# Raw weight pieces in four places instead of three, with every engine's instructions laid in a new order

## The chip, the cores and the metric

The kernel runs on one core of a Trainium2 chip. The metric is the device time of one execution in microseconds (us), the lower the better. A core has five engines that run side by side and wait for each other through semaphores: TensorE (PE; PEld is its weight load), VectorE (DVE), ScalarE (ACT), GpSimd (POOL) and SyncE (SP, which only issues the transfers here). SBUF is the on-chip memory and PSUM the memory that PE writes.

## The reference

Attention over 768 positions (4 batches, 8 heads, head size 64) with a band of 96 positions and 8 global ones, and behind it a feed-forward layer of 512 to 2048 to 512 with a piecewise quadratic in place of a GELU:

```python
scores = 0.125 * q @ k.T - slope * dist          # kept where global or local, else -1e9
a = softmax(scores)                              # by row
x = (a @ v) laid out as (4 * 768, 512)
h = x @ w_in                                     # 3072 x 2048
g = where(h >= 1, h, where(h <= -1, 0, (h + 1) ** 2 / 4))
out = g @ w_out                                  # 3072 x 512
```

w_in and w_out come as 64-bit floats, everything else as 32-bit floats.

## The kernel before

**Work.** The rows are cut into 24 units of 128 (one block of one batch) and 12 chunks of two units. A unit's attention is `scores` (PE), `masked` (DVE), `expo` and `split_p` (ACT, DVE), a transposing transfer `turn_p`, `attend` (PE), `scale_x`, `split_x` and `turn_x`. The first four units take another path (`first_...`) in which everything is in 32 bits. For a chunk c and a group g of 256 of the 2048 inner columns come `ffn1` (PE, 24 matmuls into a PSUM tile h), `gelu` (ACT step 0, DVE steps 1 and 2, then ACT and POOL), and `ffn2` (chunks 0 to 2) or `first_products` and `last_products` (later chunks, which use sums and differences of w_out that `diff` makes). Each 32-bit factor is split into a high and a low 16-bit part, so a product takes three matmuls.

**The weights.** w_in and w_out come in 32 pieces of 512 KB, 16 each. Piece n is loaded by `w_load` (an SP transfer) as raw 64-bit words into one of three places of the tile `wd`, `n % 3`. Then `w_bits` makes 32-bit floats of it: on DVE a first step (L532), a second one (L536, or for the pieces marked "s" in `WS`, which are 2, 5, 8, 11 and 14, an ACT step, L534) and a third one (L540). The first two write a PSUM tile (`w_bits`, or `spare` for the odd pieces of w_in), the third writes the result into another part of `wd`. The "s" pieces have a POOL step more, `w_sign` (L547), which still reads the raw place. `w_hi` and `w_scale` (ACT, L553, L560) and `w_lo` (POOL, L567) then give the two 16-bit parts that PE uses. A raw place can take its next piece once the last reader of the piece in it is done: the third DVE step, or `w_sign`.

**Order.** Nothing is left to a scheduler. Every step has a number, by its time in a plan, and `PLACE` is the list of these numbers in the order in which the program is written. An engine runs its own instructions of that list in that order; SP too, so a transfer that waits for its place holds up those behind it. `SLOTS` says, for each kind of tile, which buffer each tile takes. `filler` steps are PE matmuls without use that stand where PE has nothing else to do.

`wd` has eight parts: 0 to 2 are the raw places, 3 to 6 hold the 32-bit pieces, and 7 holds `own_bias`, which the `masked` steps of the first four units read. Later `diff` writes all eight.

Of the kernel before, what the change touches and what calls it, by code (L numbers as in the profile page):

```python
# [11 lines left out]
I32 = mybir.dt.int32  # L12
# [329 lines left out]
def fast_path(ctx, tc, q, k, v, nraw, nval, w_in, w_out, out, half, one, stat, marks, badi):  # L342
# [221 lines left out]
    def w_lo(n):  # L564
        num, src, hi, lo = piece(n)
        after(("hi", n), ("scale", n))
        nc.gpsimd.tensor_sub(lo, wf[n], hi)  # L567
        did.add(("w", n))

    def put_weight(n, t, tl):  # L570
        at(tl, w_load, n)
        at(t, w_bits, n, 0)
# [910 lines left out]
```

## Time and profile before

| | |
|---|---|
| runs | 593.86 us median of 3 (592.65 to 594.44) |
| the profiled execution | 592.99 us, span of its instructions 591.1 us |
| TensorE clock granted | 1.00 up to 575 us |
| busy share of the span | PE 97%, POOL 85%, DVE 80%, ACT 74% |

Times within the profile are counted from the start of the span. PE is counted busy from the start of a matmul to a modelled end; fillers count as busy.

### The profile page before, as it was taken

What the parts mean: (1) busy time and instruction counts of PE and PEld (TensorE: products, weight loads), DVE (VectorE), ACT (ScalarE), POOL (GpSimd) and SP (SyncE); (2) the same over time, 40 slices, a digit from 0 to 9 for tenths busy, and PEclk for the clock granted to TensorE, in tenths of its full rate; (3) what the DMA queues carried; (4) which work ended last, traced back from release to release, by engine and by line L of the source; (5) the groups of instructions that cost most, each with busy time, mean ns of one, the idle gap of its engine ahead of it and who ended that gap; (6) DMA issues with size and microseconds to landing.
All of it is one profiled execution on the core that took longest, in us unless ns stands there. A gap on an engine that the chain in (4) does not pass through costs nothing.

```text
span 591.1 us, 16452 instructions
## 1 busy us (share of the span) xinstructions
PE 571.7 (97%) x6243; PEld 475.7 (80%) x6243; DVE 473.5 (80%) x1175; ACT 440.2 (74%) x1146; POOL 502.2 (85%) x570
## 2 busy tenths in 40 slices
PE   7998999899999999999999999999999999999995
PEld 5876764457768688988888889888889889898884
DVE  8998999999884788787987987888979877874321
ACT  5998898998866798776976877868868768635340
POOL 0888999879999999899899998799899799579780
PEclk9999999999999999999999999999999999999999
DMA  7875675694840557848865777767667677250001
GB/s 248 279 247 189 203 238 185 144 173 88 191 105 2 114 129 153 179 127 197 196 160 129 171 176 155 179 172 188 169 150 170 158 172 171 56 123 1 2 37 42
DMA packets 144235, 88.19 MB, mean 149 GB/s; under 512 B 108180, under 2 KB 124820, under 8 KB 144148
## 3 DMA queue, kind: packets, MB, share of 16 engines
q1 hardware_dynamic: 144144, 87.05, 59.1%
q8 instruction: 51, 0.84, 0.6%
q14 instruction: 36, 0.29, 0.2%
q10 hardware_dynamic: 4, 0.00, 0.0%
HBM read 54.53 MB, written 6.29 MB: 103 GB/s over the span
## 4 chain that ended last, share of the span: by engine, by line
PE 66%; DVE 11%; ACT 10%; DMA 5%; POOL 4%; issue 3%; ACTq 0%; SPq 0%; DVEq 0%; POOLq 0%
PE h L939 30%; PE o L1042 26%; ACT z L644 5%; PE s L813 4%; PE av L854 4%; PE o L998 3%; DMA wd<-in_moe_w_out_dram 2%; DMA wd<-in_moe_w_in_dram 2%; DVE wd L540 2%; DVE u L964 1%; DVE h L962 1%; ACT ph L827 1%; POOL ga L972 1%; DVE w_bits L536 1%; DVE ph L829 1%
## 5 line engine op out<-in xcount | busy, mean ns | idle before, releaser
L939 PE MATMUL h<-xt,wih 128*128 128x256 f16 x1536 | 256.0, 273 | 5.0 <-DVE u L964 4.9
L939 PE MATMUL h<-xt,wil 128*128 128x256 f16 x768 | 209.3, 273 | 0.0
L939 PEld LDWEIGHTS <-wih 128*128 128x128 f16 x1536 | 148.4, 98 | 29.2 <-DVE u L964 9.9
L962 DVE SCALAR_TENSOR_TENSOR h<-h,u 128x512 f32<-128x512 f32 x96 | 66.4, 692 | 42.1 <-ACT u L958 41.6
L644 ACT ACTIVATE z<-z,stat 128x256 f32<-128x256 f32 (+1 forms) x192 | 91.5, 479 | 9.2 <-DVE stat L632 9.1
L983 POOL TENSOR_TENSOR ga<-u,ga 128x512 f16<-128x512 f32 x72 | 88.3, 1227 | 10.1 <-ACT ga L981 9.8
L1042 PEld LDWEIGHTS <-ga 128*128 128x128 f16 x864 | 83.2, 98 | 10.0
L958 ACT ACTIVATE u<-h,half 128x512 f32<-128x512 f32 x96 | 65.1, 678 | 33.0 <-PE h L939 22.6
L939 PEld LDWEIGHTS <-wil 128*128 128x128 f16 x768 | 75.2, 98 | 8.7
L974 POOL TENSOR_TENSOR u<-u 128x256 f32<-128x256 f32 x72 | 60.2, 838 | 20.0 <-DVE u L964 18.9
L988 POOL TENSOR_TENSOR gb<-u,gb 128x384 f16<-128x384 f32 x72 | 72.0, 1002 | 3.7 <-ACT gb L986 3.7
L1042 PE MATMUL o<-wd,ga 128*128 128x256 f16 x432 | 70.7, 273 | 0.0
L1042 PE MATMUL o<-woh,ga 128*128 128x256 f16 x288 | 70.7, 273 | 0.0
L1042 PEld LDWEIGHTS <-gb 128*128 128x128 f16 x648 | 62.3, 98 | 8.4 <-issue 1.0
L981 ACT ACTIVATE ga<-u 128x512 f16<-128x512 f32 x72 | 44.4, 621 | 33.2 <-POOL u L976 26.6
L964 DVE SCALAR_TENSOR_TENSOR u<-u,h 128x512 f32<-128x512 f32 x96 | 65.2, 680 | 3.6
L829 DVE SCALAR_TENSOR_TENSOR ph<-z,ph 128x1024 f16<-128x1024 f32 x40 | 57.0, 1428 | 9.4 <-ACT ph L827 9.0
L632 DVE CUSTOM_DVE_ANT_0 z<-s,bias 128x256 f32<-128x256 f32 x160 | 59.1, 414 | 5.1 <-PE s L813 4.7
L998 PE MATMUL o<-woh,ga 128*128 128x512 f16 x192 | 61.4, 379 | 0.6 <-ACT ob L1115 0.6
L1042 PE MATMUL o<-wd,gb 128*128 128x256 f16 x432 | 60.6, 273 | 0.8 <-DVE ob L1093 0.8
L998 PEld LDWEIGHTS <-ga 128*128 128x128 f16 x288 | 27.3, 98 | 30.6 <-issue 2.2
L599 DVE TENSOR_REDUCE stat<-c_raw 128x1 f32<-128x256 f32 x128 | 48.5, 406 | 4.3 <-DMA c_raw<-in_moe_w_in_dram 4.3
(132 smaller groups left out, 1172.2 us busy)
## 6 DMA issues: line engine op xcount, KB each, us to landing
wd<-in_moe_w_in_dram SPq DMA_DIRECT2D x16, 512.0 KB, 4.5
wd<-in_moe_w_out_dram SPq DMA_DIRECT2D x16, 512.0 KB, 4.2
c_raw<-in_moe_w_in_dram SPq DMA_DIRECT2D x32, 256.0 KB, 3.0
c_raw<-in_moe_w_out_dram SPq DMA_DIRECT2D x32, 256.0 KB, 3.4
kr<-in_k_dram SPq DMA_DIRECT2D x28, 256.0 KB, 3.6
vr<-in_v_dram SPq DMA_DIRECT2D x28, 256.0 KB, 3.6
qr<-in_q_dram SPq DMA_DIRECT2D x24, 256.0 KB, 3.9
out_dram<-ob SPq DMA_DIRECT2D x23, 256.0 KB, 3.1
```

The source lines that it names most:

```text
L632: nc.vector.tensor_tensor_reduce(out=p32[u, hf][:, hh, :], in0=pts[u, hf][hh // 2][:, hh % 2, 0:n], in1=(own_bias if n == P else bias)[:, ...
L644: nc.scalar.activation(z, z, AF.Exp, bias=nm[:, c : c + 1], scale=-1.0, accum_out=sums[:, c : c + 1])
L829: nc.vector.scalar_tensor_tensor(phs[u, hf][:, 1, :], zf, SP_, phs[u, hf][:, 0, :], op0=ALU.mult, op1=ALU.subtract)
L939: nc.tensor.matmul(hp[:, :, e, :], w[:, dc, f], xt[:, hf, 2 * a + j, :], start=(n == 0), stop=(n == 3 * NDC - 1),)
L958: nc.scalar.activation(u, h, AF.Relu, bias=half, scale=2.0 / (SV * SW), accum_out=su[:, col : col + 1])
L962: nc.vector.scalar_tensor_tensor(h, h, 4.0 / (SV * SW), u, op0=ALU.mult, op1=ALU.max)
L964: nc.vector.scalar_tensor_tensor(u, u, 4.0, h, op0=ALU.min, op1=ALU.mult)
L974: nc.gpsimd.tensor_sub(f[:, 3:7:3], f[:, 0:6:5], f[:, 4:5].to_broadcast([P, 2, P]))
L983: nc.gpsimd.tensor_sub(gas[c, g][:, 1], f[:, 0:4], gas[c, g][:, 0])
L988: nc.gpsimd.tensor_sub(gbs[c, g][:, 1, 0:3], f[:, 4:7], gbs[c, g][:, 0, 0:3])
L998: nc.tensor.matmul(po, a, w[:, f, :], start=(f == 0 and n == 0), stop=(f == NFC - 1 and n == 2))
L1042: nc.tensor.matmul(acc[:, e], x, w, start=first and n == 0, stop=last and n == 2)
```

## The change

Pieces 0 to 8 keep the three places. From the tenth piece (n = 9) on, raw pieces take four places in turn: 7, 0, 1, 2. Place 7 is the one that `own_bias` holds for the first four units. `PLACE` and `SLOTS` are new lists: all engines' instructions stand in a new order, and tiles take other buffers. The list names 36 fillers where it named 37. The other new code (`WL`, `GM`, `square`) chooses variants that the values given (`"p"` and `"d"`) never take, so that apart from the filler the instructions are the same ones.

```diff
 PLACE = [
...
-    0, 2, 1, 10, 13, 8, 20, 11, 4, 29, 3, 5, 6, 7, 89, 90, 91, 31, 15, 21, 16, 19, 18, 14, 38, 30, 39, 43, 34, 41, 26,
...
+    0, 2, 1, 10, 13, 8, 20, 11, 4, 3, 5, 6, 7, 89, 90, 91, 21, 12, 31, 9, 14, 15, 23, 22, 29, 27, 26, 25, 30, 24, 18,
...
 SLOTS = {
...
-    "raw": [int(n, 16) for n in "1001100110100110101011000110100011010010101100011010010011010100"],
+    "raw": [int(n, 16) for n in "0101010101101001010110010101100100101101000101101010001010100100"],
...
+R4 = 9
+GM = "d"
+WL = "pppppppppppppppppppppppppppppppp"
...
     def w_load(n):
         num, src, hi, lo = piece(n)
-        r = wd[:, n % 3].bitcast(I32).rearrange("p t a b -> p (t a b)")
+        r = wd[:, n % 3 if n < R4 else (7, 0, 1, 2)[(n - R4) % 4]].bitcast(I32).rearrange("p t a b -> p (t a b)")
...
     def w_lo(n):
         num, src, hi, lo = piece(n)
-        after(("hi", n), ("scale", n))
-        nc.gpsimd.tensor_sub(lo, wf[n], hi)
         did.add(("w", n))
+        if WL[n] == "v":
+            after(("hi", n))
+            nc.vector.scalar_tensor_tensor(lo, wf[n], SW, hi, op0=ALU.mult, op1=ALU.subtract)
+        else:
+            after(("hi", n), ("scale", n))
+            nc.gpsimd.tensor_sub(lo, wf[n], hi)
...
+    def square(c, g):
+        return GM[min(c * (NFC // 2) + g, len(GM) - 1)] == "s"
```

On DVE, around piece 16 (first piece of w_out), the order before has the third step of piece 13, whose place piece 16 takes, seven rows ahead of the first step of piece 16. A tile `w16_bits` belongs to piece 16; the four rows with `spare1` are the third step of piece 13 and the steps of piece 15; h and u are gelu steps.

```order
L540 SCALAR_TENSOR_TENSOR wd_117<-wd_117,spare1_172 128x512
L964 SCALAR_TENSOR_TENSOR u1_1_810<-u1_1_810,h1_1_746 128x2x256
L532 TENSOR_SCALAR w14_bits_826<-wd_117 128x512
L962 SCALAR_TENSOR_TENSOR h0_3_783<-h0_3_783,u0_3_823 128x512
L540 SCALAR_TENSOR_TENSOR wd_117<-wd_117,w14_bits_826 128x512
L532 TENSOR_SCALAR spare1_172<-wd_117 128x512
L964 SCALAR_TENSOR_TENSOR u0_3_823<-u0_3_823,h0_3_783 128x2x256
L536 SCALAR_TENSOR_TENSOR spare1_172<-wd_117,spare1_172 128x512
L532 TENSOR_SCALAR w16_bits_903<-wd_117 128x512
```

With the change piece 16 takes the place of piece 12, and on DVE the third step of piece 12 stands nine rows ahead of the first step of piece 16 (`spare1` is piece 13 here).

```order
L543 SCALAR_TENSOR_TENSOR wd_117<-wd_117,w12_bits_736 128x512
L982 SCALAR_TENSOR_TENSOR u0_2_768<-u0_2_768,h0_2_691 128x2x256
L535 TENSOR_SCALAR w14_bits_784<-wd_117 128x512
L535 TENSOR_SCALAR spare1_170<-wd_117 128x512
L980 SCALAR_TENSOR_TENSOR h1_1_740<-h1_1_740,u1_1_777 128x512
L539 SCALAR_TENSOR_TENSOR spare1_170<-wd_117,spare1_170 128x512
L982 SCALAR_TENSOR_TENSOR u1_1_777<-u1_1_777,h1_1_740 128x2x256
L543 SCALAR_TENSOR_TENSOR wd_117<-wd_117,spare1_170 128x512
L543 SCALAR_TENSOR_TENSOR wd_117<-wd_117,w14_bits_784 128x512
L980 SCALAR_TENSOR_TENSOR h0_3_790<-h0_3_790,u0_3_828 128x512
L535 TENSOR_SCALAR w16_bits_865<-wd_117 128x512
```

The first steps of pieces 16 and 15 have changed places, and the place is freed two DVE steps earlier.

On SP, from the load of piece 7 on, the order before is this; the rows named wd are the loads of the pieces, one after the other, the others are 256 KB of k, q or v of a unit.

```order
L518 DMA wd_117<-in_moe_w_in_dram 128x4x256
L746 DMA kr4_1_483<-in_k_dram 128x512
L746 DMA kr4_0_512<-in_k_dram 128x512
L518 DMA wd_117<-in_moe_w_in_dram 128x4x256 x2
L746 DMA qr4_1_599<-in_q_dram 128x512
L746 DMA vr4_0_603<-in_v_dram 128x512
L518 DMA wd_117<-in_moe_w_in_dram 128x4x256 x3
```

With the change, the same loads from piece 7 on (the first row is pieces 7 to 10, the fourth pieces 11 to 14):

```order
L521 DMA wd_117<-in_moe_w_in_dram 128x4x256 x4
L754 DMA kr5_2_552<-in_k_dram 128x512
L754 DMA qr4_1_560<-in_q_dram 128x512
L521 DMA wd_117<-in_moe_w_in_dram 128x4x256 x4
L754 DMA vr5_2_726<-in_v_dram 128x512
L754 DMA kr4_0_731<-in_k_dram 128x512
```

Four loads of pieces stand in a row, with two transfers of 256 KB right behind them, where there were one to three with two transfers between.

## Rows read from the trace of the kernel before

**Rows 1.** The head of the page, and busy time by engine.
```profile
span 591.1 us, 16452 instructions
PE   571.7 (97%) x6243; PEld 475.7 (80%) x6243; DVE 473.5 (80%) x1175; ACT 440.2 (74%) x1146; POOL 502.2 (85%) x570
```

**Rows 2.** Busy time in three stretches: length, busy us by engine, clock, DMA share, GB/s.
```profile
20.00:110.00 90.00, 82.78 (x681) 59.25 (x682) 85.06 (x184) 82.86 (x203) 81.17 (x78) 1.00 0.67 208
110.00:575.00 465.00, 463.35 (x5364) 396.50 (x5362) 367.95 (x891) 343.40 (x893) 415.83 (x483) 1.00 0.59 137
575.00:591.10 16.10, 9.70 (x89) 8.28 (x86) 2.86 (x8) 0.38 (x1) 1.36 (x2) 0.91 0.12 39
```

**Rows 3.** PE's fillers from 20 to 110 us: group of instructions, busy us, mean ns.
```profile
L494 PE MATMUL spare<-zeros 128*128 128x512 f16 x25 | 6.9, 379 | 0.0
```

**Rows 4.** PE's waits from 20 to 110 us: total us, times, longest.
```profile
PE h L939 <- DVE u L964: 3.5, 5, 1.1
PE s L813 <- DVE wd L540: 1.3, 1, 1.3
PE o L998 <- POOL wol L567: 0.6, 1, 0.6
```

**Rows 5.** PE in time, 42 to 62 us: start, length, instruction, idle before.
```profile
49.90 0.81 PE L494 MATMUL spare<-zeros 128*128 128x512 f16 x3
51.78 0.39 PE L939 MATMUL h<-xt,wih 128*128 128x256 f16 x2 [1.07 <-DVE u L964]
...
57.39 1.03 PE L494 MATMUL spare<-zeros 128*128 128x512 f16 x4
59.41 0.39 PE L939 MATMUL h<-xt,wih 128*128 128x256 f16 x2 [1.00 <-DVE u L964]
```

**Rows 6.** DVE's waits for transfers of weights, over the whole span.
```profile
DVE w_bits L532 <- DMA wd<-in_moe_w_out_dram: 2.0, 3, 1.0
DVE w_bits L532 <- DMA wd<-in_moe_w_in_dram: 1.1, 2, 0.6
DVE spare L532 <- DMA wd<-in_moe_w_in_dram: 0.8, 1, 0.8
```

**Rows 7.** DVE in time around the first step of piece 16 (56.28 us).
```profile
50.45 0.67 DVE L540 SCALAR_TENSOR_TENSOR wd<-wd,spare 128x512 int32<-128x512 int32 x1
51.05 0.67 DVE L964 SCALAR_TENSOR_TENSOR u<-u,h 128x512 f32<-128x512 f32 x1
...
54.62 0.68 DVE L536 SCALAR_TENSOR_TENSOR spare<-wd,spare 128x512 int32<-128x512 int32 x1
56.28 0.69 DVE L532 TENSOR_SCALAR w_bits<-wd 128x512 int32<-128x512 int32 x1 [0.98 <-DMA wd<-in_moe_w_out_dram]
```

**Rows 8.** The line that issues the loads of pieces: time to landing.
```profile
DMA to landing us min/median/max: 3.4/4.3/5.5
```

**Rows 9.** SP's longest wait by line: us in total, times, longest.
```profile
SPq L518 <- DVE wd L540: 42.9, 20, 3.8
```

**Rows 10.** Busy time from 20 to 40 us, columns as in rows 2.
```profile
20.00:40.00 20.00, 19.39 (x161) 15.86 (x162) 19.41 (x61) 20.00 (x60) 17.75 (x20) 1.00 0.84 270
```

**Rows 11.** POOL's `w_sign` steps from 20 to 105 us.
```profile
L547 POOL TENSOR_TENSOR wd<-wd 128x512 f32<-128x512 f32 x5 | 6.5, 1295 | 3.4 <-DVE r L656 1.4 <-ACT wd L534 1.4 <-ACT wih L553 0.6
```

**Rows 12.** All engines in time, 103 to 108 us: the steps of piece 31.
```profile
103.39 0.68 DVE L540 SCALAR_TENSOR_TENSOR wd<-wd,w_bits 128x512 int32<-128x512 int32 x1
...
105.31 0.61 ACT L553 ACTIVATE woh<-wd 128x512 f16<-128x512 f32 x1
...
105.95 0.63 ACT L560 ACTIVATE wd<-wd 128x512 f32<-128x512 f32 x1
...
106.66 1.15 POOL L567 TENSOR_TENSOR wol<-wd,woh 128x512 f16<-128x512 f32 x1 [1.36 <-ACT wd L560]
...
107.86 0.38 PE L998 MATMUL o<-wol,ga 128*128 128x512 f16 x1 [0.59 <-POOL wol L567]
```

More of the change, by code (lines that the diff above doesn't have):

```diff
@@ L107 @@
 PLACE = [
[158 rows of a table removed]
[158 rows of a table added]
 ]
 SLOTS = {
-    "ga": [int(n, 16) for n in "b469a7318025bc4943c798b07251a839bc460ab7130259cb6a5704b6b1873a590642c8304bc7531a29b0652852b7a34c01698564a086b27c456a935b91745082ac7b62b3b715c62a8b490c3498132b6a0749c640"],
-    "h": [int(n, 16) for n in "11011010111010101010101010010101010101001101110101010010010101010110101010010110101010101010110100101010100"],
-    "in": [int(n, 16) for n in "13520432105435124013454021350215423105314352141054212541013012134231524535142052"],
-    "k": [int(n, 16) for n in "201201021020120120120120"],
+    "ga": [int(n, 16) for n in "91236c504b798a317ab9674328b0c6974a23c52913b80762ac89b461b9563a7251405382c5b681a4723c0577835a619bc72486c52c09a3b1547c8b4528649a01bc26713210843b27169b2a1526841907ab343c50"],
@@ L272 @@
+    "h": [int(n, 16) for n in "10100110111010101010101010101010101010101001001010101010011011010110100101010001010101010110110011010101010"],
+    "in": [int(n, 16) for n in "23105320451235102413214503503245445012350452315404235145320542341053402431450241"],
+    "k": [int(n, 16) for n in "201120102101201202102102"],
     "kg": [int(n, 16) for n in "0000"],
-    "o": [int(n, 16) for n in "101001101010101001100101101001010110010110101"],
-    "ob": [int(n, 16) for n in "02102202001010021202010121100110"],
@@ L275 @@
-    "ph": [int(n, 16) for n in "00011010101001010110101010100101010101011010"],
-    "pt": [int(n, 16) for n in "010110111010100101100101010110011001011001100110"],
-    "q": [int(n, 16) for n in "01010110100101010110"],
-    "r": [int(n, 16) for n in "011010100110110111011001011010100110100101010101"],
-    "raw": [int(n, 16) for n in "1001100110100110101011000110100011010010101100011010010011010100"],
-    "s": [int(n, 16) for n in "0231213102031232131203120313120301233321330103101210120103212301303210331210320213312010201312231003012300102320321001012323213003321001031222012323230112021313210302123031302113021322"],
@@ L281 @@
-    "u": [int(n, 16) for n in "21212012011201211202102100210202120102102011021020102102102102101201202120120120120102102021002021021021"],
-    "v": [int(n, 16) for n in "012100201201212010201201"],
-    "x": [int(n, 16) for n in "101001010110100110111001101011000110011010010110"],
-    "xh": [int(n, 16) for n in "1010100101100110010101011010100110101001"],
-    "xt": [int(n, 16) for n in "011010101010"],
-    "z": [int(n, 16) for n in "101010101011010101001011001011001100101101001"],
+    "o": [int(n, 16) for n in "010110100101010101010101101010101010010110101"],
@@ new lines @@
+    "ob": [int(n, 16) for n in "02102112200101200202212001201021"],
+    "ph": [int(n, 16) for n in "01000101011010010110100101011010011010101010"],
+    "pt": [int(n, 16) for n in "101001011010100101101010100111011001101010011010"],
+    "q": [int(n, 16) for n in "01010010101001010101"],
+    "r": [int(n, 16) for n in "101011011001011000000101011001011010010100101001"],
+    "raw": [int(n, 16) for n in "0101010101101001010110010101100100101101000101101010001010100100"],
+    "s": [int(n, 16) for n in "0231203120103221032023120310123003213201032132103323030032101230223102330313203012032101230132102331201300123010230100021302132020021302320113130231321032102312201331102303120312201332"],
@@ L287 @@
+    "u": [int(n, 16) for n in "22102102100210120101202100210020120102102011201202120120120120120120210212010210210210210201220201201021"],
+    "v": [int(n, 16) for n in "120012010210202101210210"],
+    "x": [int(n, 16) for n in "101001001001011010011011101000010001010110101001"],
+    "xh": [int(n, 16) for n in "0110101011100101101001011010011010100101"],
+    "xt": [int(n, 16) for n in "010101010101"],
+    "z": [int(n, 16) for n in "101001010100101010110010101100110101001010110"],
 }
@@ L581, in put_weight @@
         at(t + WO[0], w_hi, n)
-        at(t + WO[1], w_scale, n)
+        if WL[n] != "v":
+            at(t + WO[1], w_scale, n)
         at(t + WO[2], w_lo, n)
@@ L946, in fast_path @@
     gas, gbs = {}, {}
+    def square(c, g):
+        return GM[min(c * (NFC // 2) + g, len(GM) - 1)] == "s"
     def gelu(c, g, s):
-        after(("g", c, g, (None, 0, 1, 2, 3, 4, 4, 6, 5, 8)[s])) if s else None
+        after(("g", c, g, (None, 0, 10 if square(c, g) else 1, 2, 3, 4, 4, 6, 5, 8, 1)[s])) if s else None
         did.add(("g", c, g, s))
@@ L960, in gelu @@
             )
+        elif s == 1 and square(c, g):
+            nc.gpsimd.tensor_scalar(u, u, 4.0, 1.0, op0=ALU.min, op1=ALU.mult)
+        elif s == 10:
+            nc.scalar.activation(u, u, AF.Square)
+        elif s == 2 and square(c, g):
+            nc.vector.scalar_tensor_tensor(u, h, 16.0 / (SV * SW), u, op0=ALU.mult, op1=ALU.max)
         elif s == 1:
@@ L1160, in put_ffn1 @@
             at(t + GEL[s], gelu, c, g, s)
+            if s == 1 and square(c, g):
+                at(t + GEL[1] + 0.6, gelu, c, g, 10)
     def put_ffn2(c, ts, g, t):
```

314 rows, old and new, of the table PLACE are left out of this document.

## The prediction

> **What bounds the kernel now.** I read the head of the page first. PE is busy for 571.7 of 591.1 us [rows 1], so the question is where the other 20 us are, and how much of the busy time is without use. The view by stretches says it: from 110 to 575 us PE idles 465.00 - 463.35 = 1.65 us, and from 20 to 110 us 90.00 - 82.78 = 7.22 us [rows 2]. In that early stretch 25 fillers take another 6.9 us [rows 3]. So of PE's time about 14 us are lost between 20 and 110 us, and hardly any later: behind 110 us the end is set by PE's own work, and whatever PE reaches earlier at 110 us the whole kernel can end earlier. Before 20 us and behind 575 us the kernel starts up and drains; I come back to these.
>
> What PE waits for in the early stretch is DVE: the feed-forward matmuls wait 3.5 us for the second DVE step of a gelu, which frees their PSUM tile, and one scores step 1.3 us for a third weight step [rows 4]. In time, this is a block of fillers and then about 1 us of idleness, again and again [rows 5]. And DVE is busy 85.06 of these 90 us [rows 2]. It idles 4.94 us, and 2.0 + 1.1 + 0.8 = 3.9 us of that, in six waits, are waits for a raw piece to land [rows 6]. Hence early on DVE sets the pace, and its only sizeable loss is late loads.
>
> Why they are late is seen at piece 16 [rows 7]. Its place is free when the third step of piece 13 ends, about 51.1 us. Seven DVE steps, 0.6 us apart (51.05 - 50.45), stand between: 4.2 us. A load takes 3.4 to 5.5 us from issue to landing, 4.3 in the middle [rows 8]. This one took about 5.1, and DVE stood for 0.98 us. Twenty loads waited on SP for such a third step, 42.9 us together [rows 9]: each is issued as soon as its place is free, so the place is what holds it.
>
> **The change, part by part.** *Four places.* Piece n now follows n - 4, not n - 3. For every piece I counted the DVE work from the third step of the piece that frees the place to the first step of the piece that takes it, 0.6 us a step (less for the small ones, by their own rows). Before, 17 of the 23 pieces from 9 on have 4.2 to 4.9 us, around the median landing and under the longest. In the new order 21 of the 22 pieces from 10 on have 5.4 us or more; the exception is piece 23, with 4.85. Piece 16 has nine steps, 5.4 us. Where an "s" piece frees the place, `w_sign` follows by 1.3 us [rows 11]; the three such pieces (12, 15, 18) keep at least 5.8. Piece 9 takes the part of `own_bias`, whose last reader stands about 8.3 us of DVE work ahead of its first step, so that this new wait is covered. If landings stay as they are, all six waits go: 3.9 us.
>
> *Loads that are let out together.* The new order puts pieces 7 to 10 and two 256 KB transfers in a row on SP. Pieces 8, 9 and 10 and those two come free within about 1.4 us of each other: 2.1 MB. At 0.84 share the transfers moved 270 GB/s [rows 10], 321 at full share, so 512 KB is 1.6 us and the other 2.7 us of a median landing are fixed. If they are served one after the other, piece 10 waits for 8 and 9: 4.3 + 2 x 1.6 - 1.4 = 6.1 us against some 6.0 of DVE work, 0.1 us late. If all five share the engines evenly, it is 2.7 + 2.1/0.321 - 1.4 = 7.8 us, 1.8 late. Two smaller bunches (piece 14 with two transfers; 16 with 15) are 1.05 MB: 4.3 in order and 2.7 + 3.3 = 6.0 shared, against 5.4: 0 to 0.6 each. With piece 23 (4.85 against at most 5.5, 0 to 0.65), what is left of the waits lies between 0.1 and 3.65 us. I take 0.7, near the lower end: one SP queue issues them all in turn, and the stretch with the highest traffic, rows 10, has 0.59 us of DVE idle in all (20.00 - 19.41).
>
> The Trainium skill (DMA: Bandwidth & Descriptors, section "Issuing engines are not separate DMA queues") has transfers run on the same 16 engines and interleave; taken as even sharing it speaks for the upper end, a gain of about 0.3 us. No row of this trace shows two pieces of such a bunch landing, so I leave it as a rival.
>
> *Same DVE work ahead.* Up to the third step of piece 31 the new order has as many DVE steps of the same kinds as the old one, 222, about 97 us by their rows. It moves single ones, most by less than 2.5 us, one gelu step by about 6. So nothing is bought there but the waits: DVE reaches that step 3.9 - 0.7 = 3.2 us earlier.
>
> *Passing it on to PE.* At the third feed-forward pair PE waits for a gelu step that keeps its position on DVE, so its 1.00 us of idleness and the fillers ahead of it [rows 5] shrink by what DVE has saved by then, 2.9 of the 3.9 us. At the end of the stretch the chain is piece 31: third step, w_hi, w_scale, w_lo, then PE [rows 12]; it hangs on DVE and moves with it. What could stop it: ACT idles 7.14 and POOL 8.83 us in the stretch [rows 2], more than the 3.2 they are to lose, and w_lo of piece 31 itself follows 1.36 us of POOL idleness [rows 12]. PE itself would have room, 14 us. So 3.2 us arrive at 110 us.
>
> *The rest.* The orders behind 110 us shift steps by up to 10 us of PE work, and which tile takes which buffer. PE idles only 1.65 us there, so little can be won; POOL is busy 415.83 of 465 us, DVE 367.95, ACT 343.40 [rows 2], so all have room to follow. I take 0, with -1.0 to +1.0. At the start DVE begins with other heads and POOL with another piece; the first scores still wait for the same loads: 0, with 0.3 either way. One filler less is 0.3 us of PE time where PE waits anyway: 0. At the end the last matmuls are the same ones, 0.
>
> **Sum.** 592.99 - 3.9 + 0.7 = 589.8 us against the profiled execution. The median of the runs, 593.86, is 0.87 higher, and the loads of a run land at random; I put the forecast 0.2 higher, at 590.0. Its own range is 588.3 to 591.7: leftover waits 0.1 to 1.5 and the two open terms.
>
> **Rivals.** *Given back on POOL and ACT.* Both run at 90 to 92% in the stretch [rows 2]; the new order also moves unit 4's first k conversions on POOL ahead of weight steps. If they become the bound half way, half the gain stays: 591.6 (590.8 to 592.6). For it: POOL has only 8.83 us of idleness in 90, ACT 7.14. Against: their waits are mostly for DVE, and go with it.
>
> *No change: the bunches share.* All upper ends above together, 3.65 us of waits, leave 0.3: 592.7 to 593.9. For it: 0.84 share already from 20 to 40 us. Against: only three places.
>
> *Slower: the clock.* In the new order the filler blocks ahead of the second and third pair (42.5 and 49.9 us) are one filler each, where four and three stood. PE then idles there unless DVE is as early as planned. Idle of 1.07 us left the clock at 1.00 [rows 5, 2]; only the last stretch, where PE idles 6.4 us, is at 0.91 [rows 2]. It decides from an idle time beyond the 1.07 seen. Three fillers take 0.81 us and four 1.03 [rows 5], so one of 512 columns is 0.22, and the 24 matmuls of 256 columns of a feed-forward step 2.6 us. At 1.2 GHz in place of 2.4 they would take 5.2; two such steps are 5.2 us more, 590.0 + 5.2 = 595.2.
>
> **How the numbers follow.** The forecast has 0.66, given back 0.17, no change 0.12, slower 0.05. About 0.3%, 1.8 us, is what a measurement of this kernel can tell from no change, so "faster" ends at 592.1. Faster: nearly all of the first and two thirds of the second, 0.65 + 0.11 + 0.01 = 0.77; the same: 0.01 + 0.06 + 0.10 = 0.17; slower: 0.05 and the edge of the third, 0.06. The range runs from 587.8 (all waits gone, and the later idleness too) to 592.8, which holds the second case, some of the third and leaves out less than 2 in 10.
>
> **What the profile would show.** Right: no DVE wait of over 0.7 us for a load of wd, under 1.0 us in all; DVE reaches the third step of piece 31 at about 100 us instead of 103.4, and fewer microseconds of fillers and idleness on PE from 20 to 110 us, about 11 in place of 14. Wrong: waits for loads at pieces 10, 14 or 16 again; or these gone, but w_lo steps on POOL without idleness ahead of them and PE waiting for the line of w_lo; or a granted clock under 1.00 near 45 us.

## The result and the profile after

The changed kernel is 0.9% slower: 598.71 us in the median of 4 runs (598.03 to 599.46) against 593.25 us (591.63 to 594.44); the ratio is 1.009, its 95% interval 1.0069 to 1.011. The forecast was 590.0 us.

The profiled execution took 599.46 us, its span is 597.7 us. The view by stretches shows in two rows where the time went (columns as in rows 2):

```profile
20.00:110.00 90.00, 85.19 (x697) 60.34 (x697) 88.59 (x192) 85.73 (x213) 85.59 (x82) 1.00 0.70 220
110.00:575.00 465.00, 455.15 (x5289) 388.89 (x5288) 359.28 (x881) 339.51 (x878) 404.50 (x472) 1.00 0.60 134
```

In the early stretch, which the prediction worked out, DVE is busy for 88.59 us in place of 85.06 and PE idles 4.81 us in place of 7.22 [rows 2]; with its 25 fillers, 7.4 us, that is 12.2 us in place of 14.1, where the prediction had about 11. Behind 110 us PE idled 1.65 us before; now it idles 465.00 - 455.15 = 9.85 us. The clock is at 1.00 in both.

Against the profile of before, a gain did arrive at 110 us. These are the third step of piece 31 on DVE and the first matmul behind its w_lo, in the views in time of DVE and of PE, against 103.39 and 107.86 us before [rows 12]:

```profile
101.30 0.68 DVE L543 SCALAR_TENSOR_TENSOR wd<-wd,w_bits 128x512 int32<-128x512 int32 x1
```
```profile
105.83 0.38 PE L1016 MATMUL o<-wol,ga 128*128 128x512 f16 x1 [0.31 <-POOL wol L575]
```

So PE was 107.86 - 105.83 = 2.0 us ahead there, and 592.99 - 2.0 + (9.85 - 1.65) = 599.2, against the 599.46 of this execution. The lead of 2.0 us rests on the one profile that it is taken against: in a second execution of the kernel before (experiment 9) the same two steps came at 100.95 and 105.36 us, ahead of the change. The loss behind 110 us stands against both, 8.2 us against the first and 9.85 - 2.27 = 7.6 us against the second. It is what has to be explained. PE's waits there, from 110 to 575 us (total us, times, longest):

```profile
PE h L947 <- DVE u L982: 4.8, 4, 1.6
PE av L862 <- DMA pt<-ph: 2.0, 2, 1.3
PE o L1060 <- POOL ga L1001: 2.0, 1, 2.0
PE av L862 <- DVE stat L640: 0.6, 2, 0.4
PE s L821 <- DVE df L1046: 0.5, 1, 0.5
```

Seven waits of over 0.6 us make most of it: 1.64 us at `ffn1 2 4` (153.7 us), 0.94 at `ffn1 2 6` (164.6; before 0.88 too), 0.76 at `ffn1 5 6` (294.7), 1.96 at `first_products 5 5` (311.8), 0.67 at `attend 14 0` (319.0), 1.42 at `ffn1 8 0` (405.7) and 1.30 at `attend 19 1` (442.5). A step is named by its function with its arguments, here chunk and group, or unit and half.

How such a wait comes about is read backwards from PE. This is the view in time of all engines before the wait at `first_products 5 5`:

```profile
291.33 5.29 SPq L844 DMA_TRANSPOSE pt<-ph  x2
...
301.55 1.05 SPq L754 DMA_DIRECT2D vr<-in_v_dram  x2
...
305.79 0.63 ACT L760 ACTIVATE vh<-vr 128x512 f16<-128x512 f32 x1 [2.77 <-DMA vr<-in_v_dram]
...
306.45 0.69 DVE L770 SCALAR_TENSOR_TENSOR vh<-vr,vh 128x512 f16<-128x512 f32 x1 [1.96 <-ACT vh L760]
...
307.43 0.92 POOL L1006 TENSOR_TENSOR gb<-u,gb 128x384 f16<-128x384 f32 x1 [3.22 <-ACT gb L1004]
```
```profile
311.80 0.28 PE L1060 MATMUL o<-wd,ga 128*128 128x256 f16 x1 [1.96 <-POOL ga L1001]
```

The reader is to see one late transfer go through four engines. `fetch 14 v 1` (v of unit 14) stands on SP behind two `turn_p`, which hold SP for 5.29 us, and four more transfers. It is issued at 301.55; ACT had been free for it since 305.79 - 2.77 = 303.02. ACT stands for 2.77 us, DVE for 1.96, POOL for 3.22, since its next gelu step waits for ACT, and then PE. Its place had been free since 273.8 us. The wait at 405.7 us is alike: v of unit 19 is issued at 393.52, ACT waits for it, and DVE waits 1.36 us for a piece that a `check_reduce` reads; from there up to the gelu step that PE needs, DVE has one gap of 0.48 us.

(`check_load` reads each piece of the weights a second time, in two halves, behind 200 us; two `check_reduce` steps on DVE take its largest and smallest magnitude.) Over the whole stretch from 110 to 575 us DVE and ACT wait for such transfers, in their waits:

```profile
DVE stat L607 <- DMA c_raw<-in_moe_w_out_dram: 7.0, 6, 2.4
DVE stat L607 <- DMA c_raw<-in_moe_w_in_dram: 6.2, 6, 3.0
```
```profile
ACT vh L760 <- DMA vr<-in_v_dram: 4.8, 2, 2.8
```

Before, DVE's waits for c_raw were 4.3 us in that stretch, and ACT had none for v. (The sum for c_raw alone doesn't set the time: e1, a faster kernel, has 5.6 us of it.) I counted how far ahead of its reader each transfer is issued (from its issue on SP to the start of its first reader, less the reader's wait for it). Of 63 check loads 16 had under 4.5 us before, some 25 have it now. The shortest lead of a `turn_p` was 4.95 us and is 3.6. The transfers land as before, in 3.3 us (c_raw), 3.6 (v, k, q; 3.4 before) and 4.6 (`turn_p`; 4.7 before) in the middle.

### The profile page after: what moved, and what is told of

Read it like the earlier page. It is cut to its first block, busy times and chain, and to the rows that moved or that the text cites. A ratio compares the mean times of both kernels' runs of the same rounds, so it can differ in the third digit from the quotient of the medians.

```text
span 597.7 us, 16476 instructions
## 1 busy us (share of the span) xinstructions
PE 573.0 (96%) x6242; PEld 475.3 (80%) x6242; DVE 469.6 (79%) x1175; ACT 441.5 (74%) x1146; POOL 499.2 (84%) x570
## 4 chain that ended last, share of the span: by engine, by line
PE 61%; DVE 14%; POOL 7%; DMA 6%; ACT 6%; issue 4%; SPq 1%; DVEq 0%; ACTq 0%; POOLq 0%
PE h L947 29%; PE o L1060 22%; PE av L862 3%; PE s L821 3%; PE o L1016 3%; DVE z L640 2%; DMA wd<-in_moe_w_in_dram 2%; DMA pt<-ph 2%; DVE ph L837 2%; DMA vr<-in_v_dram 1%; DVE u L982 1%; DVE h L980 1%; ACT u L970 1%; POOL ga L990 1%; POOL wd L1051 1%
## 5 line engine op out<-in xcount | busy, mean ns | idle before, releaser
L652 ACT ACTIVATE z<-z,stat 128x256 f32<-128x256 f32 (+1 forms) x192 | 91.8, 480 | 14.1 <-DVE stat L640 13.7
L1060 PEld LDWEIGHTS <-ga 128*128 128x128 f16 x864 | 83.2, 98 | 12.3 <-POOL ga L1001 2.2
L1001 POOL TENSOR_TENSOR ga<-u,ga 128x512 f16<-128x512 f32 x72 | 86.2, 1201 | 6.0 <-ACT ga L999 4.8
L640 DVE CUSTOM_DVE_ANT_0 z<-s,bias 128x256 f32<-128x256 f32 x160 | 60.5, 413 | 2.5 <-PE s L821 2.1
L607 DVE TENSOR_REDUCE stat<-c_raw 128x1 f32<-128x256 f32 x128 | 50.0, 408 | 13.5 <-DMA c_raw<-in_moe_w_out_dram 7.0
L1060 PE MATMUL o<-wd,gb 128*128 128x256 f16 x432 | 58.6, 273 | 0.3 <-DVE ob L1111 0.3
L1004 ACT ACTIVATE gb<-u 128x384 f16<-128x384 f32 x72 | 36.5, 514 | 24.1 <-POOL u L996 17.7
```

The source lines that it names most:

```text
L640: nc.vector.tensor_tensor_reduce(out=p32[u, hf][:, hh, :], in0=pts[u, hf][hh // 2][:, hh % 2, 0:n], in1=(own_bias if n == P else bias)[:, ...
L652: nc.scalar.activation(z, z, AF.Exp, bias=nm[:, c : c + 1], scale=-1.0, accum_out=sums[:, c : c + 1])
L1001: nc.gpsimd.tensor_sub(gas[c, g][:, 1], f[:, 0:4], gas[c, g][:, 0])
L1060: nc.tensor.matmul(acc[:, e], x, w, start=first and n == 0, stop=last and n == 2)
```

## The experiments

All ratios are to the kernel before, on the same chip, with 95% intervals; e1 to e4 and e13 to e15 ran on one chip, e5 to e12 on another. **Theory A**: the loss sits in the new order behind 125 us, **B**: in the places or the early order. Later **L**: transfers issued too shortly ahead of their readers, **O**: the order of the compute steps by itself. Orders were joined as lists: a number of steps of one list, then all other steps in the order of the other; tiles keep the buffers of their own list, but for one or two that were swapped.

**1. Places alone** (e1, repeated as e15).

```diff
 # PLACE, SLOTS and the 37 fillers of before
-r = wd[:, n % 3]
+r = wd[:, n % 3 if n < 9 else (7, 0, 1, 2)[(n - 9) % 4]]
```

> The order of before in full, with its buffers and fillers; only the raw pieces from the tenth on take four places. Theory A (the places do in the early stretch what the prediction said; the loss of the change sits in the new order behind 125 us): the six waits of DVE for pieces go, the third step of piece 31 comes about 3 us earlier, the run ends 2 to 3.5 us earlier, ratio about 0.995. Theory B (the places themselves cost, by loads that share the engines or by later work that finds its transfers late): no gain or a loss, ratio 1.000 to 1.009.

Measured: 0.9978 (0.996 to 0.9995). DVE has no wait for a piece at all. From 20 to 575 us:

```profile
20.00:110.00 90.00, 86.24 (x701) 61.15 (x701) 89.23 (x193) 86.08 (x214) 83.73 (x80) 1.00 0.70 217
110.00:575.00 465.00, 462.69 (x5368) 396.85 (x5367) 364.24 (x887) 341.36 (x886) 414.96 (x482) 1.00 0.58 136
```

> The first run once more (the order of before, four places), to narrow its interval. If the gain is that of DVE's waits for pieces, which were 3.9, 2.6, 1.3 and 0.3 us in four traces with three places (2.0 on average) and 0.0 and 0.2 us in two with four: 1 to 2 us less than before, ratio 0.9965 to 0.9985. Rival (no gain that can be measured): 0.9985 to 1.001.

Measured: 0.9986 (0.9969 to 1.0003). The places gain about 1.1 us (the mean of both), a third of the forecast of 3.2, at the edge of what can be measured. Theory A stands in that the places don't make the loss; the 2 to 3.5 us that it gave them aren't there.

**2. New early order, old rest** (e2, joined at 126 us, and e8, at 107 us).

```diff
-PLACE = [ the list of before ]
+PLACE = [ the first 723 (e8: 611) steps of the change's list, then the others as before ]
```

> The new order, with four places, up to the scores step of unit 7 (about 126 us), and from there on the order and the buffers of before. Theory A: keeps the 1.5 us that PE has gained there (126.1 against 127.6 us for the same work) and loses nothing behind it: 1.0 to 2.0 us faster than before, ratio about 0.997. Theory B (the new early order, or what it leaves behind, makes the later waits): slower, up to the full 5.5 us, ratio 1.003 to 1.009.

Measured: 0.9999 (0.9978 to 1.002).

> As the second run, but joined earlier, at the first ffn2 step of chunk 1 (107 us in the change, 109.7 us before), where the two orders have the same steps behind them but four. The second run had a wait of PE of 2.1 us for a transposed x at the join, which neither order has by itself. Theory: without that wait the new early order is as good as the old one with four places, 1 to 2.5 us faster than before, ratio 0.996 to 0.998. Rival: the new early order is no better than the old one with three places, ratio 0.999 to 1.002.

Measured: 0.9994 (0.9976 to 1.0012). Neither is slower, so the early part doesn't make the later waits; but the gain isn't there either. In e2 2.1 us went at the join. In e8 DVE waits at the bunch of loads on SP:

```profile
35.95 0.69 DVE L509 TENSOR_SCALAR w_bits<-wd 128x512 int32<-128x512 int32 x1 [1.37 <-DMA wd<-in_moe_w_in_dram]
```

The row is piece 8, issued at 30.20, which landed after 5.7 us; piece 9, issued at 30.62, landed after 6.7 and piece 10, issued at 31.21, after 7.5. What made the first of them late is taken up below, in the part on the bunch.

**3. Old early order, new rest** (e3, joined at the same point as e2, three places).

> The order of before with three places up to the same point, and the new order behind it. Theory A: slower than the change itself, since the gain of 1.5 us is missing and the later waits stay: 6 to 8 us slower than before, ratio 1.010 to 1.013. Theory B: the later waits go with the early part, ratio 0.999 to 1.003.

Measured: 1.0123 (1.0098 to 1.0148). PE's waits from 110 to 575 us are those of the change:

```profile
PE h L921 <- DVE u L956: 4.6, 5, 1.3
PE av L836 <- DMA pt<-ph: 1.9, 2, 1.2
PE h L921 <- DMA xt<-xh: 1.1, 1, 1.1
PE o L1034 <- POOL ga L975: 0.8, 1, 0.8
```

All seven are there, within a few us of their times in the change, the one at `first_products 5 5` with 0.8 us in place of 2.0; the third row is the join's. The new rest loses its time by itself.

**4. A short stretch of the new order** (e4: 304 to 344 us only, steps 1643 to 1875).

> The order of before with three places, with the new order in one stretch alone, from the third first_products step of chunk 5 (about 304 us) to the first attend step of unit 15 (about 344 us). In this stretch PE falls back by 2.9 us in the profile of the change. Theory A1 (a wait is made by the rows of the order right around it): 2 to 3 us slower than before, ratio about 1.004 to 1.005. Theory A2 (a wait needs what earlier rows left, transfers and conversions that stand later all along): within 0.7 us of before.

Measured: 1.0004 (0.9987 to 1.0021), and no PE wait in the stretch. The v of unit 14 that is late in the change had by then been issued, in the old order. So the rows around the wait at `first_products 5 5` don't make it alone; what stands ahead of them has to be there too. That this is SP's order isn't shown by e4, but by e6 and e9.

**5. Checks that don't wait** (e5), **v earlier** (e6), **both** (e7).

```diff
 # e5, e7: check_reduce reads a constant
-tops[n, e]
+bias[:, 0:2].rearrange("p a (x t) -> p (a x) t", t=2)[:, :, 1]
 # e6, e7: SP's order; v of unit 19 in the same way ahead of turn_p 17 0
+fetch 14 v 1
 turn_p 13 0
 turn_p 13 1
...
 turn_x 12 1
-fetch 14 v 1
```

> The change itself, in which each check step on DVE reads a constant of the same shape and stride in place of the piece of weights that it checks (the limits of the verdict are widened to pass it): the same DVE work and the same transfers, but no wait of DVE for a c_raw transfer, and no wait of a c_raw transfer for a check step. Theory L (the loss behind 125 us comes from transfers that are issued too shortly ahead of their readers): the 13.5 us of DVE waits for c_raw go; of PE's later waits the one at ffn1 8 0 (1.4 us) and part of those at ffn1 5 6 and first_products 5 5 go, 1.5 to 3.5 us less than the change, ratio to before 1.003 to 1.007. Theory O (the order of the DVE, ACT and POOL steps themselves makes the waits, the late transfers lie in slack): as the change, ratio 1.008 to 1.011.

Measured: 1.0026 (1.0012 to 1.0039).

> The change itself, with two transfers moved forward on SP: v of unit 14 (part 1) ahead of the two turn_p of unit 13, and v of unit 19 (part 0) ahead of the two turn_p of unit 17; their places have been free for 28 and 22 us. Theory L: ACT's waits of 2.8 and 2.1 us for them go, and with them most of the 2.0 us at first_products 5 5 and up to half of the 1.4 us at ffn1 8 0: 1 to 2.5 us less than the change, ratio to before 1.005 to 1.007. Theory O: as the change, ratio 1.008 to 1.011.

Measured: 1.0037 (1.0018 to 1.0056).

> Both edits together: checks that read a constant, and the two v transfers moved forward. Theory L: of the PE waits behind 250 us (0.8, 2.0, 0.7, 1.4 and 1.3 us, 6.1 in all) 3.5 to 6 us go; left is the wait at ffn1 2 4 (about 150 us, 1.6 us), ahead of the first check: ratio to before 0.999 to 1.004. Theory O: as the change, ratio 1.008 to 1.011.

Measured: 1.0008 (0.9993 to 1.0023): of the 0.9% nearly all is back. PE's waits in e7 from 110 to 575 us:

```profile
PE h L921 <- DVE u L956: 2.6, 2, 1.6
PE av L836 <- DMA pt<-ph: 1.0, 1, 1.0
PE s L795 <- DVE df L1020: 0.5, 1, 0.5
```

The waits at `ffn1 5 6`, `first_products 5 5`, `attend 14 0` and `ffn1 8 0` are gone; the first row is `ffn1 2 4` and `ffn1 2 6`, ahead of the first check, the second `attend 19 1`. The stretch from 110 to 575 us in e5, e6 and e7:

```profile
110.00:575.00 465.00, 459.68 (x5336) 393.64 (x5335) 358.02 (x881) 341.07 (x882) 409.26 (x476) 1.00 0.60 134
110.00:575.00 465.00, 458.58 (x5315) 391.29 (x5314) 362.62 (x888) 341.60 (x885) 408.30 (x475) 1.00 0.61 135
110.00:575.00 465.00, 460.23 (x5340) 393.91 (x5339) 358.54 (x883) 341.89 (x882) 409.97 (x478) 1.00 0.59 134
```

PE idles 5.32, 6.42 and 4.77 us there, in place of 9.85. Either edit alone removes the waits at `first_products 5 5`, `attend 14 0` and `ffn1 8 0`; e6 does it although DVE still waits 12.3 us for c_raw, so those waits alone don't make PE wait there. In e5 ACT still waits once for v, 1.37 us. Two transfers alone (e6) give back 1.0090 - 1.0037, 0.53% or about 3 us. O is out for these four waits; for `ffn1 2 4` and `ffn1 2 6`, which stay in all three, it isn't.

**6. The opposite: v later in a good order** (e9, on e1).

```diff
 # SP's order, old list with four places
-fetch 14 v 1
...
 turn_x 13 1
+fetch 14 v 1
 turn_x 13 0
...
-fetch 19 v 0
...
 turn_p 18 0
+fetch 19 v 0
```

> The order of before with four places (the first run), with two transfers moved back on SP: v of unit 14 (part 1) behind the first turn_x of unit 13, and v of unit 19 (part 0) behind the first turn_p of unit 18. In the first run they were issued 17.7 and 6.4 us ahead of their readers; now they are issued at about 300.8 and 401.4 us, when the readers on ACT stand at 299.3 and 400.9. Theory L (transfers issued too shortly ahead of their readers are enough to make PE wait): ACT waits about 5 and 4.5 us, PE loses 2 to 6 us against the first run, ratio to before 1.001 to 1.008. Theory O (a late v lies in slack): as the first run, 0.996 to 0.9995.

Measured: 1.0125 (1.0105 to 1.0145), some 8.5 us above e1: more than expected. ACT's view in time has both waits, and the view by stretches PE's clock around the second:

```profile
306.46 0.63 ACT L734 ACTIVATE vh<-vr 128x512 f16<-128x512 f32 x1 [5.53 <-DMA vr<-in_v_dram]
...
411.18 0.63 ACT L734 ACTIVATE vh<-vr 128x512 f16<-128x512 f32 x1 [3.77 <-DMA vr<-in_v_dram]
```
```profile
410.60:413.05 2.45, 0.07 (x1) 0.00 (x0) 0.54 (x1) 1.87 (x5) 0.00 (x0) 1.00 1.15 270
413.05:413.30 0.25, 0.25 (x2) 0.11 (x2) 0.25 (x2) 0.25 (x1) 0.22 (x1) 1.00 1.30 248
413.30:413.50 0.20, 0.15 (x2) 0.00 (x0) 0.20 (x1) 0.20 (x2) 0.20 (x1) 0.55 1.28 283
414.20:420.00 5.80, 5.71 (x27) 4.08 (x28) 5.69 (x12) 2.61 (x9) 5.64 (x9) 0.50 0.16 45
```

From 110 to 575 us PE idles 9.9 us, 7.6 more than in e1, and the half clock costs some 2.9 us of this execution (half of the 5.71 busy ones). It is the slowest of six, 603.07 us with a mean clock of 0.991; the other five took 599.62 to 602.91 us at 0.995 to 0.997, so the clock took less of them. Two late transfers out of 281 on SP are enough to cost this kernel about as much as the whole change did.

**7. A looser bunch** (e10, on e8: q of unit 4 goes ahead of the load of piece 8, k of unit 5 behind that of piece 12).

> As the eighth run (the new early order up to 107 us), with two 256 KB transfers taken out of the bunch on SP: q of unit 4 (part 1) goes ahead of the load of piece 8, k of unit 5 (part 2) behind the load of piece 12; their places are free from 28.4 and 30.5 us on. Theory S (the loads of pieces 8 to 10 and the two transfers share the engines, which is where the gain of the new early order went): DVE's waits at pieces 8 and 10 (1.4 and 0.3 us) fall to 0.3 to 0.9 us together, 0.7 to 1.5 us are won, ratio to before 0.997 to 0.999. Rival (the loads of the pieces are late by themselves): waits of over 1.2 us stay, ratio 0.998 to 1.001.

Measured: 0.9987 (0.997 to 1.0004). The wait at piece 8 fell from 1.37 to 0.47 us, that at piece 10 stayed (0.32), and new ones stood at pieces 14 (0.88) and 23 (0.54), with 2.2 us in all. Inconclusive: the interval holds both forecasts, and the wait at piece 8 is anywhere from 0 to 1.8 us in traces of the same early order.

**8. One gelu step forward** (e11, on e7).

```diff
 # DVE's order
 gelu 2 2 1
 masked 8 1 3
+gelu 2 2 2
 split_x 6 1 1
 diff 4 0
 diff 4 2
 norm 7 1
-gelu 2 2 2
```

> As the seventh run (the change with checks that read a constant and two v transfers forward), with one DVE step moved forward: the second DVE step of gelu of chunk 2, group 2 goes ahead of the split of x of unit 6 (second half), which with two diff steps had stood between its two steps. The wait of PE at ffn1 2 4 (1.65 us) is ahead of the first check, so late transfers can't make it. Theory D (the order of DVE's own steps makes it): it falls to under 0.3 us, 1.0 to 1.7 us less than the seventh run, ratio to before 0.997 to 0.9995. Rival (DVE gives it back at the next gelu step): ratio 1.000 to 1.002.

Measured: 1.0013 (0.9993 to 1.0032). The rival was right: the wait at `ffn1 2 4` is gone, but that at `ffn1 2 6` grew from 0.94 to 2.26 us. What DVE does ahead of these two steps delays one or the other; one step's place doesn't cure it.

**9. The kernel before, once more** (e12).

> The kernel before, unchanged: another execution's trace. In the profile of before DVE waited 3.9 us for pieces in six waits; in the two other traces with the same early order and three places (the third and fourth run) it was 0.3 and 2.6 us. Theory: the sum is drawn anew in each execution, anywhere from 0.3 to 4 us, and the third step of piece 31 comes between 101.0 and 103.5 us. Rival: 3.9 us is usual and the joined kernels are earlier for another reason: 3.5 to 4.3 us, piece 31 at 103 to 104 us.

Measured: 0.9999 (0.9972 to 1.0025); the profiled execution took 590.57 us, with piece 31 at 100.95 us, the first matmul behind its w_lo at 105.36, and these waits of DVE for pieces:

```profile
DVE w_bits L532 <- DMA wd<-in_moe_w_out_dram: 0.8, 2, 0.5
DVE w_bits L532 <- DMA wd<-in_moe_w_in_dram: 0.6, 1, 0.6
```
```profile
105.36 0.38 PE L998 MATMUL o<-wol,ga 128*128 128x512 f16 x1 [0.58 <-POOL wol L567]
```

Four traces of the old early order with three places have 3.9 [rows 6], 2.5 (e4), 1.4 (e12) and 0.5 us (e3) of such waits, 2.1 on average. With four places it is 0.0, 0.2, 0.2 and 0.7 (e1, e9, e15, e14), 0.3 on average. The new early order with four places has 0.5 to 2.3, 1.4 on average, in eight traces (the change, e2, e5 to e8, e11 and e13).

**10. Checks at the places of before** (e13), **and the old early order ahead of that** (e14). e13 is e6 with each check step behind as many other steps of the list as before, reading its piece again. e14 takes the first 611 steps from the list of before.

> The change with nothing left out: v of units 14 and 19 forward on SP as in the sixth run, and the load and the two DVE steps of every check of the weights at the places in the list that they have before (behind as many other steps). In the fifth and seventh run the checks read a constant, which also freed the c_raw transfers from waiting for them; here only their places change. Theory L: DVE's waits for c_raw fall from 13.5 us to 3 to 7, and the time to that of the seventh run, ratio to before 0.999 to 1.003. Rival (in the fifth and seventh run the gain came from SP, which no longer waited for checks): as the sixth run, ratio 1.003 to 1.006.

Measured: 1.0069 (1.0045 to 1.0092).

> The order of before with four places up to the first ffn2 step of chunk 1 (about 107 us), and behind it the mended order of the thirteenth run. Theory: the early order of before with four places is worth about 1 us against the new one, and what is left of the new order's later waits (3.5 us at ffn1 2 4, ffn1 2 6 and attend 19 1 in the seventh run against 1.4 us in the first) still costs 1 to 2 us against the first run: ratio to before 0.998 to 1.002. Rival (the two rests are equal once the transfers are mended): as the first run, 0.996 to 0.998.

Measured: 1.0092 (1.0066 to 1.0118). Both missed. In e13 DVE's waits for c_raw did fall to 3.0 us, and the waits at `first_products 5 5`, `attend 14 0` and `ffn1 8 0` are gone. But there are new ones: 1.18 us at `ffn1 4 5`, and two for `turn_p`, at `attend 12 1` (1.10) and `attend 13 1` (0.97). e14 has the same three, of 0.89, 1.49 and 0.87 us; PE idles 8.1 us in e13 and 8.4 in e14 from 110 to 575 us. In e13:

```profile
PE h L921 <- DVE u L956: 4.5, 5, 1.6
PE av L836 <- DMA pt<-ph: 2.3, 3, 1.1
```

SP's view in time shows the first of these two: two check loads now stand between the two `turn_p` of unit 12, which in the change followed each other (267.74, 5.53 us for both):

```profile
268.38 1.94 SPq L818 DMA_TRANSPOSE pt<-ph  x1
270.37 1.50 SPq L576 DMA_DIRECT2D c_raw<-in_moe_w_in_dram  x2
271.97 3.09 SPq L818 DMA_TRANSPOSE pt<-ph  x1
```

So, as far as these two waits go, a transfer's place counts against those around it on SP: the checks' old places fit the old order's transfers only. Whether the gain of e5 came from DVE's waits for c_raw or from SP, which no longer waited for the checks, isn't told apart by this, and stays open.

## Why the prediction was wrong

**The step that failed** is "The rest": "PE idles only 1.65 us there, so little can be won; POOL is busy 415.83 of 465 us, DVE 367.95, ACT 343.40 [rows 2], so all have room to follow. I take 0, with -1.0 to +1.0." It measured +8.2 us (7.6 against the second trace of the kernel before). Room in busy time says how much work fits, not whether each transfer is issued far enough ahead of its reader. The new list moves steps on SP past each other, and a `turn_p` or a `check_load` that waits or is slow to issue there holds up a v that three engines need. The prediction followed the loads of the pieces on SP, in the early stretch, and none of the transfers behind it. e3 shows that the loss is in that part, e5 to e7 that late transfers make most of it (5.1 of the 8.2 us go), and e9 that two of them suffice. About 1.6 us, at `ffn1 2 4`, have another cause: DVE's own order around 150 us (e11 moved that wait without curing it).

**Four places** did what was said: no wait at pieces 12, 13, 16, 26 or 30 in the change. At piece 10 one of 0.77 us is left (0.58 before), over the 0.7 that the prediction gave as the most, and one of 0.26 us at piece 6, whose place is one of three, is new. But the term was mis-sized. The 3.9 us of waits were one draw; the average of four traces is 2.1, and e1 and e15 gain about 1.1 us.

**The bunch** was on the forecast's list as a rival: loads that share the engines evenly. The traces speak against that. A load lands in 16 steps, whose times the trace keeps, and the last of them is its landing. In e8 the eighth steps of pieces 8, 9 and 10 come 3.34, 4.38 and 5.32 us after their issue, at 33.54, 35.00 and 36.53 us: 1.5 us apart, one load after the other, as in the lower of the prediction's two estimates. The Trainium skill (DMA: Bandwidth & Descriptors, section "Issuing engines are not separate DMA queues") has transfers interleave on the same 16 engines; the even sharing that I took from it isn't seen in these steps. What makes piece 8 late are its last two steps, at 4.80 and 5.72 us, where the other fourteen are there by 3.61. In 13 traces with four places its eighth step comes at 3.34 to 3.62 us and its last one at 4.05 to 6.21. Loads before the change have such stragglers too: piece 13, in the trace of rows 6, has fifteen steps by 3.68 us and the last at 5.55; piece 12 has its last step at 5.47 us there and at 3.78 in e12. So a late landing is one or two late steps out of 16, which differ from execution to execution; why they are late isn't shown. I took 0.7 us for what is left of the waits; the change itself had 1.0, eight traces 1.4 on average. With an average of 2.1 before, the new early order gains 0.7 us of DVE waits, which e2 and e8 can't tell from nothing.

**Passing it on to PE** held, 2.1 us on DVE at piece 31 and 2.0 on PE; but as a gain this was in part luck of the trace that it is taken against. In four traces of the old early order with three places that step comes at 101.9 us on average (100.95 to 103.39), in nine of the new one at 101.6 (100.48 to 102.47), and in four of the old one with four places at 100.8. *Given back on POOL and ACT* isn't seen before 110 us: PE waits 0.3 us for the line of w_lo there, 0.6 before [rows 4]. *The clock* stayed at 1.00, with one filler each at the two places, so the only rival on the slow side was the wrong one.

## What to carry to other kernels

When a whole order is laid anew, follow each transfer on its queue: from its issue to its reader's turn, against the time that such a transfer takes to land, and what stands ahead of it and may block. A stretch in which the bound engine idles hardly at all has nothing to win and everything to lose. Mending such an order by hand isn't done by that alone: e13 and e14, mended so, missed their forecasts by new waits. A sum of waits for transfers out of one profile is one draw; a second trace of the same kernel is the cheapest check on a forecast that rests on it. The change's useful part, the four places, is best taken alone (e1, e15).

## What was not expected of the hardware

In e9 PE idled for 2.38 us, up to 413.05 us, and from 413.3 us on the clock was at 0.50, 1.2 GHz, up to 420 us; a second idle time, of 0.84 us, ended behind the fall. By the rows of experiment 6 the half clock cost an estimated 2.9 us on top of these 3.2 us of waiting. The 1.96 us at `first_products 5 5` in the change left the clock at 1.00.

Pieces 6 to 31 have the eighth of their 16 landing steps 3.4 us after their issue, in the middle (the trace of rows 6). The landing hangs on the last one or two steps, and for the same piece in the same order these came up to 2.2 us earlier or later (piece 8, e13 and e6).

On SP a `turn_p` takes 1.3 to 3.7 us to issue in the change, and a pair 5.3 us, where a plain transfer of v, k or q takes 0.43 to 0.46 in the middle: what stands behind a pair on this queue is issued later by more than the 3.6 us that a v takes to land.
